# Joined-batch rows in one transfer, the last tile in one step, one x w product moved ahead

## The chip, the cores and the metric

The kernel runs on one core of a Trainium2 chip. The time is device microseconds (us) of one launch; three runs of the kernel before gave 436.42, 436.83 and 436.47 us, so its time is the median of **436.47 us**.

The engines are PE (matmul), DVE (vector), ACT (scalar), POOL (GpSimd) and SP, which only issues DMA transfers. Sixteen DMA engines move the data of all queues.

## The reference

Inputs are q, k and v of 8 batches x 8 heads x 576 positions x 64, weights `w_r` and `w_i` of 64 modes x 512 x 512, and `w_ch` of 512 x 512, all float32. Cut to what matters:

```python
rel = pos[:, None] - pos[None, :]
mask = (rel >= 0) & (rel < 64)
attn = softmax(where(mask, q @ k.T / 8, -1e9))        # sliding window, causal
x = (attn @ v) as [8, 576, 512]                       # heads side by side
X = rfft(x, axis=1)[:, :64]                           # 64 modes
Y = einsum('bmd,mde->bme', X, w_r + 1j * w_i)         # complex product
y = irfft(Y padded with zeros, n=576, axis=1)
u = x + y
out = u + maximum(u @ w_ch, 0)                        # [8, 576, 512] float32, 9.44 MB
```

## The kernel before

The work is one program with an order written out by hand (`tc.manual_schedule()`), so each engine runs its instructions in the order in which the code emits them. First comes attention, with a discrete Fourier transform of each batch as a matmul. Meanwhile and afterwards POOL's queue streams the weights `w_r` and `w_i` into rings of tiles, and `mode_half` multiplies them with the transformed x, four modes at a time. The last two groups of modes (`LAST`, `LAST + 1`) are held back as a small remainder: the outputs' share of all other modes can be prepared before them.

The output has 36 tiles of 128 rows x 512. For each batch four of them are rows 128c to 128c + 127. Rows 512 to 575 of two neighbouring batches are joined to one further tile: tiles 8, 17, 26 and 35 hold batches (0, 1), (2, 3), (4, 5) and (6, 7), the even batch in partitions 0 to 63, the odd one in partitions 64 to 127. `tiles[i]` holds the tile's x, its (column, batch) pairs and its one or two places in `out`; `tile_of` gives a tile's number.

For each tile two sums are formed in PSUM: `pu` is u = x + irfft(Y), and `ps` is u @ w_ch, made of a stored product `XW[i]` (x @ w_ch) and the transformed Z = Y @ w_ch. `tail_xw(n, js)` copies `XW` of the tiles js of pair n into `ps` with a matmul by the identity (L777); this is called the first x w product here.

The tiles go in 18 pairs, `seq`:

- n = 0 to 3: (0, 4), (1, 5), (2, 6), (3, 7);
- n = 4 to 11, alternating: (18, 19), (9, 13), (20, 21), (10, 14), (22, 23), (11, 15), (24, 25), (12, 16);
- n = 12 and 13, the joined-batch tiles, `X4`: (8, 17), (26, 35);
- n = 14 to 17, `BB`: (27, 28), (29, 30), (31, 32), (33, 34).

Tiles 0 to 7 and 9 to 16 are "early" ones. All their sums but the share of the last modes are ready beforehand, and the function `early(n)` ends them: PE adds the small remainders (L787, L794), DVE adds u (L820, `take_u`), ACT rectifies (L825) and POOL adds the two (L826, `take_z`). The others are done in full by `full_u(n)` and `full_z(n)`: PE computes the rows (L836, L840, for joined tiles L845, L859), ACT or DVE takes u from PSUM (L853, L851; for tile 28 POOL adds x, L855), and DVE rectifies and adds (L878). The last pair is done by `last(n)`, with its own DVE steps and transfers (L902, L905). Before all this, after the last weights, `zl` (L984) is the remainder's product with `w_ch` in two halves, `cast_halves` (L618, L619) takes such halves to SBUF with DVE and ACT, and pair n = 0 is written out by hand.

PSUM has eight banks in five rings, `bank(h)`: "m" two, "t" two, "z" two, "y" one, "p" one. `ps` of even pairs uses "t" and of odd pairs "z"; `pu` of even pairs uses "m", of odd pairs "y" and "p".

The output transfers follow `plan`, an order that is worked out beforehand from assumed times of each tile. SP issues the tiles in that order: ..., 11, 8, 17, 15, 26, 35, 12, 16, 27, 29, 31, 33, 34. Some transfers are given to ACT (`by_act`): the upper halves of the four joined tiles, and the whole tiles 28, 30 and 32. ACT issues them one pair later, when `full_u` or `last` of the next pair calls `send_behind` behind its own copies.

In the last pair, tile 33 is one DVE step and one transfer by SP. Tile 34 is two DVE steps of 256 columns, of which SP sends the first half and ACT the second.

Of the kernel before, what the change touches and what calls it, by code (L numbers as in the profile page):

```python
# [13 lines left out]
ALU = mybir.AluOpType  # L14
# [12 lines left out]
def kernel(  # L27
# [10 lines left out]
    nc = tc.nc  # L38
    B, H, S, D = q.shape
    NM = moe_w_r.shape[0]  # L40
    DM = moe_w_ch.shape[0]
# [7 lines left out]
    HALF = DM // 2  # L49
# [117 lines left out]
    def mode_half(psm, grp, hb, ri, first, last):  # L167
        pairs = range(4 * grp, 4 * grp + 4)
        of, p0 = (XL[hb], 4 * LAST) if grp // 2 == LAST // 2 else (XQ[hb], 0)
        order = [(j, p) for j in range(NJ) for p in pairs]  # L170
        ending = (grp, hb, ri) == (*steps[-1], 1)
        if ending:
            order.sort(key=lambda jp: (jp[1], jp[0]))
        for j, p in order:
            g = p % 4
            parts = psm if isinstance(psm, list) else [psm]
            for i, ps in enumerate(parts):
                e = DM // len(parts)
                nc.tensor.matmul(out=ps[32 * g:32 * g + 32, 0:e],  # L179
                                 lhsT=of.rearrange("k s b m -> k (s b) m")[:, (3 * j + 1 - ri) * B:(3 * j + 5 - ri) * B, p - p0],  # L180
                                 rhs=wtiles[p, hb, ri][:, j, e * i:e * i + e],
                                 start=(first and ri == 0 and j == 0), stop=(last and ri == 1 and j == NJ - 1),
                                 tile_position=(0, 32 * g))
        for p in pairs:
            wtiles.pop((p, hb, ri))
        spent.update(i for i, (_, ps, *of) in enumerate(wlist) if ps[0] in pairs and of == [hb, ri])

    with tc.manual_schedule():
# [184 lines left out]
        for nm in ("k", "q", "v"):  # L373
# [9 lines left out]
                                in1=at.unsqueeze(2).to_broadcast([128, NTF, NM]), op0=ALU.mult, op1=ALU.mult)  # L383
# [7 lines left out]
                         op0=ALU.max, op1=ALU.min)  # L391
# [141 lines left out]
        def bank(h, shape=(128, DM), dtype=FP32, name=None):  # L533
            return banks[h].tile(list(shape), dtype, name=name or "ps" + h, tag="bank")
# [196 lines left out]
        tiles = []  # L731
# [23 lines left out]
        BB = [(8, 17), (26, 35)] + [(i, i + 1) for k in range(NLB // 2, B // 2) for i in range(9 * k, 9 * k + 8, 2)]  # L755
        assert sorted(i for p in AA + BB for i in p) == list(range(NT))
        X4 = [BB.pop(0) for _ in range(2)]
        seq = [AA.pop(0) for _ in range(4)]
# [3 lines left out]
        ps, pu = {}, {}  # L762
# [9 lines left out]
        done = {}  # L772

        def tail_xw(n, js=(0, 1)):
            for i in [seq[n][j] for j in js]:
                ps[i] = bank("zt"[n % 2 == 0])
                nc.tensor.matmul(out=ps[i], lhsT=ident_r, rhs=XW[i], start=True, stop=True)  # L777

        def banks_u(n):
            for j, i in enumerate(seq[n]):  # L780
                pu[i] = bank("m" if n % 2 == 0 else "yp"[j])

        def late_u(n):
            for i in seq[n]:
                (at, b), = tiles[i][1]
                r = slice(YG[b], YG[b] + 16)
                nc.tensor.matmul(out=pu[i], lhsT=trigL[r, at:at + 128], rhs=YL[r], start=True, stop=True,  # L787
                                 tile_position=(YG[b], 0))
# [5 lines left out]
                nc.tensor.matmul(out=ps[i], lhsT=trigLr[r, at:at + 128], rhs=ZL[r], start=False, stop=True,  # L794
                                 skip_group_check=True, tile_position=(ZG[b], 0))

        by_act = {(i, 1) for p in X4 for i in p} | {(p[1], 0) for p in BB[:-1]}
        behind = []

        def send(i, ut):  # L800
            done[i] = ut
            behind.extend((i, h) for h in range(2) if (i, h) in by_act)
            while plan and plan[0] in done:
                i = plan.pop(0)
                for h in range(len(tiles[i][2])):
                    if (i, h) not in by_act:
                        put_out(nc.sync, i, h)

        def put_out(by, i, h):
            to = tiles[i][2]  # L810
            m = 128 // len(to)
            by.dma_start(out=to[h], in_=done[i][m * h:m * h + m, :])

        def send_behind():
            while behind:
                put_out(nc.scalar, *behind.pop(0))

        def take_u(n):
            for i in seq[n]:
                nc.vector.tensor_tensor(out=UE[i], in0=pu[i], in1=UE[i], op=ALU.add)  # L820
# [41 lines left out]
        uts = {}  # L862
# [17 lines left out]
                send(i, ut[:, j])  # L880

        def early(n):
            tail_xw(n)
            banks_u(n)
            late_u(n)
            late_z(n)
            take_u(n)
            take_z(n)

        def last(n):  # L890
            banks_u(n)
            ut = [ringA.tile([128, 2, DM], FP32, name="ut", tag="wt")[:, 0] for _ in range(2)]
            for j, i in enumerate(seq[n]):
                rows_u((i,))
                take_rows(i, ut[j])
            send_behind()
            for j, i in enumerate(seq[n]):
                tail_xw(n, (j,))
                rows_z(i)
                for lo in range(0, DM, HALF * (2 - j)):  # L900
                    hi = lo + HALF * (2 - j)
                    nc.vector.scalar_tensor_tensor(out=ut[j][:, lo:hi], in0=ps[i][:, lo:hi], scalar=0.0,  # L902
                                                   in1=ut[j][:, lo:hi], op0=ALU.max, op1=ALU.add)
                    by = nc.scalar if lo else nc.sync
                    by.dma_start(out=tiles[i][2][0][:, lo:hi], in_=ut[j][:, lo:hi])  # L905

        stmp2 = pool("stmp2", side="right", reuse_waits="tile")
        tables = list(inverse_tables())
# [5 lines left out]
        for i, (grp, hb) in enumerate(steps[EARLY:]):  # L914
            f, l = grp < EARLY or hb == 0, hb == 1
            if i == EARLY:
                while tables:
                    tables.pop(0)()
                while jobs or pend:
                    advance()  # L920
                close(stmp2, yp, ringB)
                Zall = pool("zall", side="right").tile([2 * NM, B, DM], FP32R, name="Zall")
                x_jobs(pool("xp1", side="right", reuse_waits="tile"), NX0, NT)
                nc.vector.memset(YT[:, :, :, rows], 0.0)
                nc.vector.tensor_scalar(out=trz.rearrange("p c g k -> p c (g k)"), scalar1=0.0, scalar2=None, op0=ALU.mult,
                                        in0=ident.unsqueeze(1).to_broadcast([128, NDCH, 128]))
                for g in range(4):
                    nc.sync.dma_start(out=trigL[32 * g:32 * g + 16], in_=trigI[rows, 0:512])
                    nc.sync.dma_start(out=trigLr.bitcast(FP32)[32 * g:32 * g + 16], in_=trigIr.bitcast(FP32)[rows, 0:512])
                given = 0  # L930
            if f:
                psm = [bank("m"), bank("m")] if grp == LAST + 1 else bank("m")
            for ri in range(2):
                if half == n0 + n1 - 2:
                    while jobs or pend:
                        advance()
                if half == n0 + n1 - 1:
                    late["first"] = bank("z")
                    late[0][1]()
                    tail_xw(0)  # L940
                mode_half(psm, grp, hb, ri, f, l)
                load_weights(len(wlist))
                while ready:
                    ready.pop(0)()
                for t in tables[0:2]:
                    t()
                del tables[0:2]
                if half == 0:
                    nc.gpsimd.dma_start(out=wch, in_=moe_w_ch.rearrange("(c p) e -> p c e", p=128))
                if l and ri:  # L950
                    finish_group(grp, psm)
                    if grp == NGRP - 1:
                        ready.pop(0)()
                        for b in range(B):
                            batch_job(b)
                            if 0 < b <= NLB:
                                early_jobs(b - 1)
                half += 1
                if half <= n0:
                    want = max(half - 4, 0) * NX0 // (n0 - 4)  # L960
                elif half <= n0 + n1 - 8:
                    want = (half - n0) * (NT - NX0) // (n1 - 8)
                else:
                    want = NT - NX0 + (half - n0 - n1 + 8) * (B + 7 * NLB) // 6
                while given < want:
                    advance()
                    given += 1
# [10 lines left out]
        YL = stgpool.tile([128, DM], BF16, name="stg")  # L978
        nc.vector.tensor_copy(out=YL, in_=first)
        take()  # L980
        zl = [bank("z"), bank("m")]
        for h, ps_ in enumerate(zl):
            for c in range(NDCH):
                nc.tensor.matmul(out=ps_[:, 0:HALF], lhsT=trz[:, c].rearrange("p g k -> p (g k)"),  # L984
# [57 lines left out]
```

## Time and profile before

| | |
|---|---|
| median of the runs | 436.47 us (436.42 to 436.83) |
| the profiled execution: its own time | 436.39 us |
| its span in the profile | 434.6 us |
| mean granted PE clock | 0.879 |
| PE busy | 339.6 us, 78% of the span |
| DVE, ACT, POOL busy | 231.7, 179.8, 144.1 us |
| software queue q0 (weights and attention inputs) | 81.73 MB, 99.7% of 16 engines' span |
| output by SP's queue | 28 transfers of 256 KB, 5 of 128 KB |
| output by ACT's queue | 3 transfers of 256 KB, 5 of 128 KB |
| last weights land, PE goes on | 397.9 us |
| last arithmetic ends | 429.3 us |

The span runs from the first to the last instruction that the profiler saw, and times inside it count from its start. A busy share is an average over stages: the weights fill the DMA queues up to about 398 us, and the part that the change touches most is what comes behind. There a line of the timeline stands for a group of instructions: its start, its length, the engine, the source line, the operation, what it writes and reads, and in brackets the idle time of the engine before it with what ended that. "SPq" and "ACTq" mark the issue of a transfer, not the transfer itself.

### The profile page before, as it was taken

Reading aid. Unit: us, or ns where it says so; the run is one execution under the profiler, and the core shown is the slowest. Engines: PE = TensorE matmul, PEld = TensorE weight load, DVE = VectorE, ACT = ScalarE, POOL = GpSimd, SP = SyncE. Lnnn points to the kernel's source line nnn. Section 1 sums busy time; section 2 is a strip of 40 time slices with the busy share of each in tenths; the row PEclk is TensorE's granted clock in tenths of the full one; section 3 lists DMA queues with packets and bytes.
Section 4 is the critical chain, followed back from the end, with each engine's and each line's share of the span. In section 5 each row is a group of like instructions: output and inputs, shape, how many; then the busy total and the mean of one; then the engine's idle time right before and its main releaser. Section 6 shows DMA issues by size and latency. Waiting matters only on the chain.

```text
span 434.6 us, 11132 instructions
## 1 busy us (share of the span) xinstructions
PE 339.6 (78%) x4758; PEld 219.3 (50%) x4802; DVE 231.7 (53%) x472; ACT 179.8 (41%) x322; POOL 144.1 (33%) x212
## 2 busy tenths in 40 slices
PE   6889989898999998986407665767696678878994
PEld 3566767676677676662103232444353345445552
DVE  8488778787677675865103111122131315662994
ACT  5566666575666667531201110121121213334842
POOL 9332323332314223223232223123332223310890
PEclk8699999999999999986558558588888989999998
DMA  8999999999999999999999999999999999993798
GB/s 205 211 211 211 212 210 210 212 210 211 211 211 211 212 212 210 211 211 211 211 258 213 216 211 211 211 211 211 211 212 212 209 211 211 211 211 71 241 367 295
DMA packets 48273, 93.65 MB, mean 215 GB/s; under 512 B 3680, under 2 KB 4128, under 8 KB 48224
## 3 DMA queue, kind: packets, MB, share of 16 engines
q0 software_dynamic: 42000, 81.73, 99.7%
q1 hardware_dynamic: 5328, 9.77, 6.4%
q10 hardware_dynamic: 896, 1.44, 1.1%
q8 instruction: 37, 0.61, 0.5%
q14 instruction: 12, 0.10, 0.1%
HBM read 163.58 MB, written 9.44 MB: 398 GB/s over the span
## 4 chain that ended last, share of the span: by engine, by line
DMA 44%; PE 38%; issue 9%; ACT 3%; DVE 3%; POOL 2%; DVEq 0%; POOLq 0%
DMA wr<-in_moe_w_r_dram 37%; PE tr L222 6%; PE s L269 5%; PE s L281 4%; PE pt L289 4%; PE vb L234 4%; DMA rawk<-in_k_dram 3%; DMA wi<-in_moe_w_i_dram 3%; PE o L309 3%; PE s L261 2%; PE psm L179 2%; POOL wi L158 1%; PE psz L777 1%; PE px L332 1%; PE pst L777 1%
## 5 line engine op out<-in xcount | busy, mean ns | idle before, releaser
L158 POOL DMA_DIRECT2D wi<-in_moe_w_i_dram x62 | 44.0, 711 | 93.0 <-PE psm L179 41.9
L601 PE MATMUL psz<-wch,tr 128*128 128x512 f32 x176 | 63.0, 491 | 11.2 <-DMA wch<-in_moe_w_ch_dram 11.0
L747 DVE CAST xw<-psz 128x512 fp32r<-128x512 f32 x36 | 24.9, 692 | 86.7 <-PE psz L601 86.1
L158 POOL DMA_DIRECT2D wr<-in_moe_w_r_dram x53 | 37.9, 716 | 83.9 <-PE psm L179 38.6
L273 DVE TENSOR_REDUCE mx<-s 128x4 fp32r<-128x512 f32 x72 | 49.5, 688 | 27.2 <-PE s L269 26.8
L575 ACT CAST tr<-ptx 128x512 fp32r<-128x512 bf16 x36 | 21.1, 587 | 103.6 <-PE ptx L594 103.6
L179 PEld LDWEIGHTS <-XQ 128*32 128x32 bf16 x448 | 20.9, 167 | 71.2 <-issue 63.8
L179 PE MATMUL psm<-wi,XQ 128*32 128x512 bf16 x212 | 28.8, 469 | 30.4 <-DMA wi<-in_moe_w_i_dram 30.4
L601 PEld LDWEIGHTS psz<-wch,tr 128*128 128x128 f32 x176 | 37.5, 236 | 18.3 <-issue 11.6
L283 ACT ACTIVATE p<-s 128x512 bf16<-128x512 f32 x72 | 39.7, 603 | 13.9 <-PE s L281 13.9
L179 PE MATMUL psm<-wr,XQ 128*32 128x512 bf16 x180 | 25.9, 497 | 17.5 <-DMA wr<-in_moe_w_r_dram 16.7
L269 PE MATMUL s<-kT,qT 64*64 64x128 bf16 (+1 forms) x576 | 29.4, 223 | 6.9 <-issue 6.9
L226 ACT COPY kT<-tr 128x576 bf16<-128x576 bf16 x32 | 23.1, 723 | 22.5 <-PE tr L222 22.5
L292 DVE COPY pts<-pt 128x1024 bf16<-128x1024 bf16 (+1 forms) x40 | 25.2, 629 | 5.9 <-PE pt L289 4.5
L226 ACT COPY qT<-tr 128x576 bf16<-128x576 bf16 x32 | 23.3, 728 | 10.5 <-PE tr L222 10.4
L269 PEld LDWEIGHTS <-qT 64*64 64x64 bf16 x576 | 18.0, 108 | 18.6 <-issue 18.0
L281 PE MATMUL s<-mx,ident_r 128*128 128x512 f32 x72 | 26.8, 445 | 0.0
L226 ACT COPY vT<-tr 128x576 bf16<-128x576 bf16 x32 | 23.3, 728 | 4.3 <-PE tr L222 4.2
L289 PE MATMUL pt<-ident_bf,p 128*128 128x128 bf16 x288 | 23.4, 220 | 2.0 <-issue 1.8
L626 DVE TENSOR_TENSOR stg<-psm,Ypair 128x512 bf16<-128x512 f32 x10 | 6.9, 690 | 33.6 <-PE psm L179 33.6
L321 DVE TENSOR_TENSOR x_sb<-o,r 128x512 bf16<-128x512 f32 x32 | 22.1, 692 | 1.1
L209 POOL DMA_DIRECT2D rawk<-in_k_dram x15 | 8.3, 556 | 39.4 <-PE tr L222 24.5
(211 smaller groups left out, 612.6 us busy)
## 6 DMA issues: line engine op xcount, KB each, us to landing
wi<-in_moe_w_i_dram POOLq DMA_DIRECT2D x60, 512.0 KB, 16.0
wr<-in_moe_w_r_dram POOLq DMA_DIRECT2D x53, 512.0 KB, 16.4
out_dram<-ut SPq DMA_DIRECT2D x28, 256.0 KB, 3.0
rawv<-in_v_dram POOLq DMA_DIRECT2D x16, 288.0 KB, 14.3
rawk<-in_k_dram POOLq DMA_DIRECT2D x15, 288.0 KB, 13.1
rawq<-in_q_dram POOLq DMA_DIRECT2D x15, 288.0 KB, 13.4
Ypair<-in_moe_w_r_dram POOLq DMA_DIRECT2D x5, 512.0 KB, 14.3
x_sb<-in_moe_w_r_dram POOLq DMA_DIRECT2D x4, 512.0 KB, 15.3
```

What stands on the lines that cost most here:

```text
L158: nc.gpsimd.dma_start(out=w[:, 0:len(ps)], in_=src[ps[0]:ps[-1] + 1, HALF * hb:HALF * hb + HALF, :].rearrange("g (p j) e -> p g j e", j=NJ))
L179: nc.tensor.matmul(out=ps[32 * g:32 * g + 32, 0:e], lhsT=of.rearrange("k s b m -> k (s b) m")[:, (3 * j + 1 - ri) * B:(3 * j + 5 - ri) * B ...
L222: nc.tensor.transpose(out=pt[ro, j, :], in_=raw[ro, TH * half + j, :], identity=ident_bf[ro, ro])
L226: nc.scalar.copy(out=to, in_=pt.rearrange("p j n -> p n j"))
L269: nc.tensor.matmul(out=s[ro, t, lo:128], lhsT=lq, rhs=kT[ro, 64 * n - 64 + lo:64 * n + 64], start=False, stop=True, skip_group_check=True)
L273: nc.vector.tensor_reduce(out=mx, in_=s, axis=AX.X, op=ALU.max, negate=True)
L281: nc.tensor.matmul(out=s, lhsT=ident_r, rhs=mx.unsqueeze(2).to_broadcast([128, 4, 128]), start=False, stop=True, skip_group_check=True)
L283: nc.scalar.activation(out=p[:, 4 * c2:4 * c2 + 4, :], in_=s, func=ACT_F.Exp, scale=EX_SCALE)
L289: nc.tensor.transpose(out=pt[:, t, :], in_=st[u]["p"][:, t, :], identity=ident_bf)
L292: nc.vector.tensor_copy(out=ps[:, 0:nt, :], in_=pt[:, 0:nt, :])
L601: nc.tensor.matmul(out=pz, lhsT=tr[:, c, :], rhs=wch[:, c, :], start=(c == 0), stop=(c == NDCH - 1))
L747: nc.vector.tensor_copy(out=XW[i], in_=multiply(tr))
```

## The change

Four things are edited.

- The joined tiles leave by pairs: one transfer of SP takes partitions 0 to 63 of both tiles of a pair (batches 0 and 2, or 4 and 6), one of ACT takes partitions 64 to 127 (batches 1 and 3, or 5 and 7). SP's is issued when the plan comes to the pair's second tile, ACT's in the next `send_behind`.
- `by_act` is gone, so tiles 28, 30 and 32 are sent by SP in the plan's order.
- The last pair: tile 34 is one DVE step of 512 columns and one transfer, by ACT.
- The first x w product of tile 1 (the first of pair n = 1) moves from `early(1)` to just ahead of the last `mode_half`, behind those of pair n = 0. It takes the second "z" bank, so the first half of `zl` takes a bank "m" in place of "z".

```diff
-        by_act = {(i, 1) for p in X4 for i in p} | {(p[1], 0) for p in BB[:-1]}
         behind = []
 
         def send(i, ut):
             done[i] = ut
-            behind.extend((i, h) for h in range(2) if (i, h) in by_act)
             while plan and plan[0] in done:
                 i = plan.pop(0)
-                for h in range(len(tiles[i][2])):
-                    if (i, h) not in by_act:
-                        put_out(nc.sync, i, h)
-
-        def put_out(by, i, h):
-            to = tiles[i][2]
-            m = 128 // len(to)
-            by.dma_start(out=to[h], in_=done[i][m * h:m * h + m, :])
+                if len(tiles[i][2]) == 1:
+                    nc.sync.dma_start(out=tiles[i][2][0], in_=done[i])
+                elif i == tiles_of_two(i)[1]:
+                    put_two(nc.sync, i, 0)
+                    behind.append(i)
+
+        def tiles_of_two(i):
+            return next(p for p in X4 if i in p)
+
+        def put_two(by, i, h):
+            p = tiles_of_two(i)
+            b = [tiles[t][1][h][1] for t in p]
+            by.dma_start(out=out[b[0]:b[1] + 1:b[1] - b[0], 512:576].rearrange("b t e -> t b e"),
+                         in_=uts[seq.index(p)][64 * h:64 * h + 64])
 
         def send_behind():
             while behind:
-                put_out(nc.scalar, *behind.pop(0))
+                put_two(nc.scalar, behind.pop(0), 1)
...
         def early(n):
-            tail_xw(n)
+            tail_xw(n, (0, 1) if n > 1 else (1,))
...
                 rows_z(i)
-                for lo in range(0, DM, HALF * (2 - j)):
-                    hi = lo + HALF * (2 - j)
-                    nc.vector.scalar_tensor_tensor(out=ut[j][:, lo:hi], in0=ps[i][:, lo:hi], scalar=0.0,
-                                                   in1=ut[j][:, lo:hi], op0=ALU.max, op1=ALU.add)
-                    by = nc.scalar if lo else nc.sync
-                    by.dma_start(out=tiles[i][2][0][:, lo:hi], in_=ut[j][:, lo:hi])
+                nc.vector.scalar_tensor_tensor(out=ut[j], in0=ps[i], scalar=0.0, in1=ut[j], op0=ALU.max, op1=ALU.add)
+                by = nc.scalar if j else nc.sync
+                by.dma_start(out=tiles[i][2][0], in_=ut[j])
...
                     late["first"] = bank("z")
                     late[0][1]()
                     tail_xw(0)
+                    tail_xw(1, (0,))
                 mode_half(psm, grp, hb, ri, f, l)
...
-        zl = [bank("z"), bank("m")]
+        zl = [bank("m"), bank("m")]
```

## The prediction

> **What bounds the kernel now.** I read the page's second part first. From the second to the 36th slice the DMA engines are over 90% busy, mostly with weights; slice 37 (71 GB/s) is the change from reading weights to writing results, and the last three slices write.
>
> ```profile
> DMA  8999999999999999999999999999999999993798
> GB/s 205 211 211 211 212 210 210 212 210 211 211 211 211 212 212 210 211 211 211 211 258 213 216 211 211 211 211 211 211 212 212 209 211 211 211 211 71 241 367 295
> ```
>
> The edit of the last weight step (the moved product) stands at 395 us, all others behind 419 us, so the second view is the windows of the end. Columns: stretch, its length, busy time of PE, PEld, DVE, ACT, POOL, then the granted clock, the DMA share and GB/s.
>
> ```profile
> 408.00:409.00 1.00, 0.95 (x9) 0.60 (x10) 1.00 (x3) 0.49 (x1) 1.00 (x2) 1.00 0.51 186
> 409.00:415.00 6.00, 6.00 (x36) 4.01 (x35) 5.36 (x10) 4.50 (x10) 6.00 (x6) 1.00 1.03 381
> 415.00:421.00 6.00, 6.00 (x32) 3.45 (x31) 5.60 (x10) 2.74 (x6) 6.00 (x6) 1.00 1.03 381
> 421.00:422.00 1.00, 1.00 (x6) 0.56 (x5) 1.00 (x2) 0.00 (x0) 1.00 (x2) 1.00 1.05 279
> 422.00:423.00 1.00, 1.00 (x6) 0.63 (x6) 1.00 (x3) 0.59 (x1) 1.00 (x1) 1.00 0.97 330
> 423.00:424.00 1.00, 0.95 (x7) 0.79 (x6) 0.90 (x2) 0.62 (x2) 1.00 (x2) 1.00 0.97 348
> 424.00:425.00 1.00, 1.00 (x8) 0.55 (x7) 0.85 (x3) 0.45 (x1) 0.20 (x1) 1.00 0.83 240
> 425.00:426.00 1.00, 1.00 (x7) 0.86 (x6) 1.00 (x2) 0.55 (x2) 0.00 (x0) 1.00 0.92 301
> 426.00:429.00 3.00, 2.33 (x13) 1.34 (x11) 2.46 (x6) 1.60 (x4) 0.00 (x0) 1.00 1.04 391
> ```
>
> PE is busy without a break until 428.3, and the chain of waits names PE there. But from 409 us on the DMA engines are full too, and they stay full (386 GB/s) from 429 to 432, when no engine computes. The timeline of the end says the same:
>
> ```profile
> 427.96 1.35 DVE L902 SCALAR_TENSOR_TENSOR ut<-psz,ut 128x512 f32<-128x512 f32 x3 [0.29 <-ACT ut L853]
> 428.68 2.27 SPq L905 DMA_DIRECT2D out_dram<-ut  x2
> 429.39 0.34 ACTq L905 DMA_DIRECT2D out_dram<-ut  x1
> ```
>
> The last arithmetic ends at 427.96 + 1.35 = 429.31, the DMA engines run to about 433, and the span is 434.6. An output transfer lands in as little as 2.3 us; the last ones need 3.7. So the end is set by the draining of result bytes, about 1.4 us behind the arithmetic, and an edit is worth what it does to that drain. The drain has one bad stretch, 421 to 426 us, in which the two pairs of joined-batch tiles (8,17) and (26,35) leave as eight transfers of 64 rows (128 KB), four from SP and four from ACT. There 300 GB/s stand against 381 before: (381 - 300) x 5 / 381 = 1.06 us lost. The DMA view splits it by queue (q1 is SP's, q10 is ACT's), first for 409 to 421, then for 421 to 426:
>
> ```profile
> q1 hardware_dynamic: 2499, 4.56, 102.7%
> ```
>
> ```profile
> q1 hardware_dynamic: 559, 0.97, 53.3%
> q10 hardware_dynamic: 316, 0.52, 41.1%
> ```
>
> A share is of 16 engines over the window. Ordinary: 1.027 x 12 x 16 / 4.56 = 43.2 us of engine time a MB. In the bad stretch SP's queue costs 0.533 x 80 / 0.97 = 44.0, with its 64-row transfers in it; ACT's costs 0.411 x 80 / 0.52 = 63.2. ACT's rows 64 to 127 are thus dear: (63.2 - 43.2) x 0.52 / 16 = **0.65 us**. The rest is idle engines: the mean share is 0.948 against 1.03, 5 x 0.082 / 1.03 = **0.40 us**. They idle while ready work stands at SP:
>
> ```profile
> 420.52 2.56 POOL L826 TENSOR_TENSOR ut<-XQ,ut 128x512 f32<-128x512 f32 x2
> ...
> 423.80 1.15 SPq L812 DMA_DIRECT2D out_dram<-ut  x1
> ```
>
> That SP row is tile 12, the first of these two POOL steps, ready near 421.8. Its transfer issues two microseconds later and takes 1.15 us to do so, behind 17's, 15's, 26's and 35's.
>
> **The change part by part.** *The joined transfers.* Eight 128 KB transfers become four of 256 KB; the same 1.05 MB from the same halves of the partitions, still lower rows by SP, upper rows by ACT. SP has 3 issues ahead of tile 12 from (8,17) on where it had 5, and each carries the bytes of an ordinary tile, so its queue should stay as full as in 409 to 421, where transfers of 256 KB alone kept it at 381 GB/s. I take the 0.40 us of idle engines as regained (bounds: 0, and a loss if the joined form is dearer, below). The dear rows of ACT stay: no row shows why they are dear, and their number doesn't change; 0.65 us stays (bounds: all regained, or SP's rows as dear). The joined form adds a wait: tile 8's rows wait for tile 17's DVE step, 0.65 us later (L878 takes 1.28 for two). Behind it on SP stand 15, 12 and 16, but the second half-transfer stood in the same place with the same wait, so they wait no longer than now; and SP's queue then still holds tile 11. On ACT the joined transfer of (26,35) waits until 422.7, as 35's does now, with the copy of tile 29 (423.38) behind it.
>
> *Tiles 28, 30, 32 from ACT to SP.* SP then sends all tiles before the last; its issue count from tile 8 on is 11 before (8, 17, 15, 26, 35, 12, 16, 27, 29, 31, 33) plus half of 34, 12, and after it 2 + 3 + 7 = 12. One queue alone moved 381 GB/s, two moved 391 (426 to 429). Over 4 us that is 1.56 / 0.381 - 1.56 / 0.391 = **0.10 us** lost. ACT loses three issues between its copies, which helps nobody: PE doesn't wait there.
>
> *The last tile.* DVE: one step of 0.68 for two of 0.33 to 0.35; the end of arithmetic stays at 429.3. SP's half was issued late, at 429.79, as SP was still busy with tile 33; now all leaves by ACT at about 429.4. With the engines full until 432 an earlier issue is worth nothing by itself. Packets of 1 KB become 2 KB: 432 to 433 us, mostly 1 KB packets, has 0.803 x 16 / 0.27 = 47.6 us a MB against 43.2, for 0.26 MB: **0.07 us** won.
>
> *The moved product.* PE loses one product of x and w (0.47 for a pair at full clock, so 0.23) from the row of n = 1, at 402.3, and gets it at about 396, where it stands 0.72 us idle ahead of the last matmuls for the last weights (L179, released by the DMA at 397.9): hidden, 0.23 if the weights came early. At 402 it is not on the path either, as ACT's rectifying steps follow one another without a gap, and PE waits for the banks that they free:
>
> ```profile
> 402.44 1.09 ACT L825 ACTIVATE ut<-pst 128x512 f32<-128x512 f32 x2
> 403.43 1.08 ACT L825 ACTIVATE ut<-psz 128x512 f32<-128x512 f32 x2
> 404.54 1.08 ACT L825 ACTIVATE ut<-pst 128x512 f32<-128x512 f32 x2
> ```
>
> The first two pairs of outputs go through POOL from 403.1 on, which starts behind the product of n = 0 as before. Value 0, at most 0.23, and hidden by the drain even then. The second bank "m" for `zl` comes free with the casts of the last group (398.9), before L984 at 399.7; the banks of n = 0 come free with the casts of `zl` (400.9, 401.4), before L787 at 401.8: nothing.
>
> *Sum.* -0.40 + 0.10 - 0.07 = -0.37 us. The profiled execution took 436.39 (434.61 and 1.78 around it), 0.08 under the median of 436.47; the median falls to **436.1**. 0.2% is 0.87 us, about what a measurement of this kernel can tell from no change.
>
> **The rivals.** *B: the whole bad stretch goes.* If ACT's rows are dear because its half transfers ran with little beside them, full queues on both sides cure that too: -1.06 + 0.10 - 0.07 = -1.03, and 435.4. For: 421.5 to 422 is the dearest half microsecond, with q10 alone at work (48 packets, 97.8% of the engines, 163 ns each, 217 GB/s). Against: from 424 to 425.5, with q1 at work too, q10's 122 packets still took 53.0% of 16 engines, 104 ns with the tiny ones counted. Only with the stretch nearly gone is it faster by over 0.87.
>
> *C: slower.* A joined transfer takes two packets from each of 64 partitions. If this makes both queues' rows as dear as ACT's worst (163 ns for 2 KB, 79.6 us a MB), the stretch loses (79.6 - 43.2) x 1.05 / 16 = 2.39 us for 1.06: +1.33 + 0.03, 437.8. It decides from a mean of 72 us a MB over all four transfers. Against: SP's lower rows show no surcharge at all. For: the transfer into few partitions, `Zall` (16 rows of the tile, 256 KB), needed 4.2 us to land where an output early in the tail needs 2.3 to 2.9.
>
> *D: nothing is regained.* The stretch runs at the rate of 64-row transfers whatever their number: 436.47 + 0.03 = 436.5. For: 64 rows are all that is special in the stretch; against, SP's cheap ones. [...]
>
> **How the numbers follow.** The forecast, idle engines regained and dear rows kept, 0.45, 436.1; B 0.27, 435.4; D 0.18, 436.5; C 0.10, 437.8. Forecast and D are within 0.2%: 0.63; B is faster: 0.27 (it and a little of the moved product); C is slower: 0.10. The range leaves out C's upper part: from B with 0.23 of the product and the scatter of runs, 435.0, to 437.0, half of C's price.
>
> **What would show it.** Right: DMA share over 1.0 through the stretch, q10 still over 55 us a MB, SP's long issue near 424 gone or earlier, 380 GB/s on q1 to the end, last arithmetic at 429.3 and the DMA end some 0.4 us earlier. Wrong: idle engines in the stretch still (D), q10 near 43 us a MB (B), q1 over 60 (C), or arithmetic that ends at another time than 429.3.

## The result, and the profile after

The changed kernel takes **437.47 us** (median of 20 runs, 436.82 to 437.79); the kernel before took 436.59 us in the same comparison (20 runs, 436.10 to 437.51). The ratio is 1.0019, 95% interval 1.0012 to 1.0026: slower by 0.9 us, where 436.1 and a range of 435.0 to 437.0 were forecast. The profiled execution took 437.57 us with a span of 435.8, 1.2 us more than the span before.

The page's second part, same two lines: up to the last slices nothing differs; slice 37 to 40 show the writing of results, with a lower rate in slice 39 (326 for 367 GB/s).

```profile
DMA  8999999999999999999999999999999999992898
GB/s 206 211 211 211 212 211 211 210 211 211 211 211 211 211 211 211 211 211 211 212 258 212 216 211 211 211 211 211 211 211 211 211 211 211 211 209 59 276 326 291
```

The windows of the end, after (stretch, length, busy time of PE, PEld, DVE, ACT, POOL, granted clock, DMA share, GB/s):

```profile
415.00:421.00 6.00, 6.00 (x31) 3.46 (x31) 5.60 (x10) 2.67 (x6) 6.00 (x6) 1.00 1.03 381
421.00:422.00 1.00, 1.00 (x6) 0.53 (x5) 1.00 (x3) 0.03 (x1) 1.00 (x2) 1.00 0.74 207
422.00:423.00 1.00, 1.00 (x6) 0.65 (x6) 1.00 (x3) 0.56 (x1) 1.00 (x2) 1.00 0.98 186
423.00:424.00 1.00, 0.95 (x6) 0.76 (x5) 0.90 (x2) 0.63 (x2) 1.00 (x1) 1.00 1.00 244
424.00:425.00 1.00, 1.00 (x7) 0.58 (x6) 0.89 (x3) 0.45 (x1) 0.10 (x1) 1.00 0.93 275
425.00:426.00 1.00, 1.00 (x7) 0.86 (x6) 1.00 (x2) 0.84 (x2) 0.00 (x0) 1.00 1.00 283
426.00:427.00 1.00, 1.00 (x9) 0.56 (x8) 0.70 (x3) 0.31 (x2) 0.00 (x0) 1.00 1.00 287
427.00:428.00 1.00, 1.00 (x7) 0.71 (x4) 0.71 (x3) 1.00 (x2) 0.00 (x0) 1.00 0.91 301
428.00:431.00 3.00, 0.26 (x2) 0.00 (x0) 1.18 (x2) 0.01 (x1) 0.00 (x0) 1.00 1.04 390
433.00:434.00 1.00, 0.00 (x0) 0.00 (x0) 0.00 (x0) 0.00 (x0) 0.00 (x0) 0.50 0.87 330
```

Up to 421 us the two kernels are alike. Then the bad stretch is both longer (to 428 instead of 426) and lower. The loss against 381 GB/s is now (381 - 255) x 7 / 381 = 2.3 us, 255 GB/s being the mean of the seven rows; it was 1.06. The engines still write at 330 GB/s at 433 us, when the kernel before was done. The timeline shows that arithmetic isn't late: it ends at 427.89 + 1.29 = 429.2 (429.3 before).

```profile
427.89 1.29 DVE L904 SCALAR_TENSOR_TENSOR ut<-psz,ut 128x512 f32<-128x512 f32 x2 [0.29 <-issue]
429.21 0.36 ACTq L906 DMA_DIRECT2D out_dram<-ut  x1
431.82 0.78 SPq L906 DMA_DIRECT2D out_dram<-ut  x1
```

The DMA view of 421 to 428 us by queue (packets, MB, share of 16 engines), after:

```profile
q1 hardware_dynamic: 686, 1.25, 63.4%
q10 hardware_dynamic: 288, 0.52, 30.2%
```

SP's queue costs 0.634 x 112 / 1.25 = 56.8 us of engine time a MB, where it was at 44.0 before; ACT's costs 65.0 (63.2 before). The shares add up to 0.94 against 1.03: 0.62 us of idle engines, for 0.40. So SP's rows are dear here, as rival C had it (though just under the 60 named as its sign), and the idle time grew. How dear a joined transfer is shows between 421.6 and 422.9 us, where one is alone:

```profile
DMA packets 119, 0.24 MB, mean 186 GB/s; under 512 B 1, under 2 KB 1, under 8 KB 119
q1 hardware_dynamic: 119, 0.24, 96.5%
```

0.965 x 1.3 x 16 / 119 = 169 ns a packet of 2 KB; an ordinary one takes 43.2 us a MB x 2 KB = 88 ns. ACT's joined transfer isn't there yet, though it was issued in the same moment:

```profile
420.26 0.67 SPq L815 DMA_DIRECT2D out_dram<-ut  x1
420.26 0.72 ACTq L815 DMA_DIRECT2D out_dram<-ut  x1
```

### The profile page after: what moved, and what is told of

Same layout as the page of the kernel before. It is cut to its first block, busy times and chain, and to the rows that moved or that the text cites. A ratio compares the mean times of both kernels' runs of the same rounds, so it can differ in the third digit from the quotient of the medians.

```text
span 435.8 us, 11120 instructions
## 1 busy us (share of the span) xinstructions
PE 340.4 (78%) x4758; PEld 220.5 (51%) x4802; DVE 230.9 (53%) x471; ACT 179.7 (41%) x322; POOL 144.0 (33%) x212
## 4 chain that ended last, share of the span: by engine, by line
DMA 48%; PE 35%; issue 8%; ACT 3%; DVE 2%; POOL 1%; DVEq 0%; POOLq 0%
DMA wi<-in_moe_w_i_dram 33%; DMA wr<-in_moe_w_r_dram 7%; PE tr L222 6%; PE s L269 5%; DMA Yall<-in_moe_w_i_dram 4%; DMA rawk<-in_k_dram 4%; PE pt L289 4%; PE s L281 3%; PE vb L234 3%; PE o L309 2%; PE s L261 2%; PE psm L179 2%; PE psz L777 1%; PE pst L777 1%; PE pst L863 1%
## 5 line engine op out<-in xcount | busy, mean ns | idle before, releaser
L179 PE MATMUL psm<-wi,XQ 128*32 128x512 bf16 x212 | 29.9, 475 | 28.6 <-DMA wi<-in_moe_w_i_dram 28.6
L179 PE MATMUL psm<-wr,XQ 128*32 128x512 bf16 x180 | 24.9, 491 | 17.2 <-DMA wr<-in_moe_w_r_dram 16.6
L222 PE MATMUL tr<-ident_bf,rawk 64*64 64x64 bf16 x576 | 15.6, 197 | 5.3 <-DMA rawk<-in_k_dram 3.3
```

The source lines that it names most:

```text
L179: nc.tensor.matmul(out=ps[32 * g:32 * g + 32, 0:e], lhsT=of.rearrange("k s b m -> k (s b) m")[:, (3 * j + 1 - ri) * B:(3 * j + 5 - ri) * B ...
L222: nc.tensor.transpose(out=pt[ro, j, :], in_=raw[ro, TH * half + j, :], identity=ident_bf[ro, ro])
```

## The experiments

All kernels are the kernel before with the edit shown, unless said otherwise. A ratio is against the kernel before on the same chip.

### One edit at a time

**The joined transfers alone** (the other edits left out):

```diff
-        by_act = {(i, 1) for p in X4 for i in p} | {(p[1], 0) for p in BB[:-1]}
+        by_act = {(p[1], h) for p in X4 for h in (1,)} | {(p[1], 0) for p in BB[:-1]}
+        two = {i: p for p in X4 for i in p}
...
-                    if (i, h) not in by_act:
+                    if (i, h) not in by_act and not (i in two and (h or i == two[i][0])):
...
+            if i in two:
+                b = [tiles[t][1][h][1] for t in two[i]]
+                by.dma_start(out=out[b[0]:b[1] + 1:b[1] - b[0], 512:576].rearrange("b t e -> t b e"),
+                             in_=uts[seq.index(two[i])][64 * h:64 * h + 64])
+                return
```

> The kernel before with the four joined transfers alone (lower rows by SP, upper rows by ACT); 28, 30 and 32 stay on ACT, the last tile stays in two halves. Theory 1 (the joined transfers are the whole loss): the stretch from 421 us runs near 255 GB/s for about 7 us as in the changed kernel, both queues over 55 us of engine time a MB there, and the kernel is slower by 0.8 to 1.3 us (ratio 1.002 to 1.003). Theory 2 (the loss comes from giving SP all other tiles): within 0.3 us of the kernel before, the stretch near 300 GB/s.

Measured: 437.90 us, ratio 1.0032 (1.0020 to 1.0045): 1.3 us slower, at the upper end of what theory 1 gave. The stretch is there again: 274 GB/s over 421 to 428 us, with both queues at 56 us of engine time a MB. Its first rows:

```profile
421.00:422.00 1.00, 1.00 (x7) 0.56 (x5) 1.00 (x3) 0.00 (x0) 1.00 (x1) 1.00 0.79 283
422.00:423.00 1.00, 1.00 (x6) 0.64 (x4) 1.00 (x3) 0.59 (x1) 1.00 (x2) 1.00 0.99 195
423.00:424.00 1.00, 1.00 (x8) 0.79 (x8) 0.90 (x2) 0.25 (x1) 1.00 (x2) 1.00 0.99 236
424.00:425.00 1.00, 1.00 (x7) 0.63 (x6) 0.86 (x2) 0.83 (x2) 0.48 (x1) 1.00 0.92 252
```

**The changed kernel with only the joined transfers undone** (eight half transfers again, the other three edits kept):

```diff
-                elif i == tiles_of_two(i)[1]:
-                    put_two(nc.sync, i, 0)
-                    behind.append(i)
+                else:
+                    put_half(nc.sync, i, 0)
+                    behind.append(i)
...
-                put_two(nc.scalar, behind.pop(0), 1)
+                put_half(nc.scalar, behind.pop(0), 1)
```

> The changed kernel with the joined transfers alone undone: eight half transfers again, lower by SP and upper by ACT; 28, 30 and 32 on SP, the last tile in one step and the moved product stay. Theory 1 (the joined transfers are the whole loss): within 0.3 us of the kernel before, ratio 0.9995 to 1.0005, the stretch near 300 GB/s. Theory 2 (the other three edits): as slow as the changed kernel, ratio 1.0019.

Measured: 436.59 us, ratio 0.9999 (0.9990 to 1.0008), and 307 GB/s from 421 to 426 us, close to the 300 of the kernel before. With the joined transfers the loss comes, without them it goes: theory 1. The three other edits by themselves:

**The moved product** (`tail_xw(1, (0,))` ahead of the last `mode_half`, `zl` in two "m" banks):

> The kernel before with the moved x w product alone (and the bank of zl with it). All theories: no effect over 0.1 us at the end, since ACT's rectifying steps pace the first pairs and the output transfers drain until 433 us; the first output transfer leaves about 0.1 us earlier, as in the changed kernel (404.34 against 404.43), and ratio 1.000 within 0.0005. If the product did cost something, this run alone would be slower by over 0.3 us.

Measured: ratio 1.0002 (0.9993 to 1.0010). The first output transfer was issued at 404.51 us, not earlier than before.

**The last tile** (one DVE step, one transfer by ACT):

> The kernel before with the last tile in one DVE step and one transfer by ACT alone. Theory 1 (the joined transfers are the whole loss): between -0.2 and +0.1 us, the last packet near 433.1. Theory 2 (the loss is at the end of the queues, where tile 33 waits on SP's queue until 431.8 us in the changed kernel): +0.3 us or more already here.

Measured: ratio 1.0001 (0.9993 to 1.0010). The DMA engines were done shortly after 433 us (0.04 busy from 433 to 434).

**Tiles 28, 30, 32 by SP** (`| {(p[1], 0) for p in BB[:-1]}` dropped):

> The kernel before with tiles 28, 30 and 32 sent by SP alone; the joined-batch tiles keep their eight half transfers. Theory 1: +0.1 us at most, 381 GB/s on one queue against 391 on two. Theory 2: slower by 0.8 to 1.2 us, as SP's issues of over 1 us each delay the last tiles.

Measured: ratio 1.0003 (0.9994 to 1.0012). None of the three can be told from no change; the bounds are 0.4 to 0.5 us, so the forecast's 0.07 and 0.10 us are neither confirmed nor refuted. Theory 2 falls. The joined transfers alone cost more (1.0032) than the whole change (1.0019), but the intervals overlap: whether the other edits give a little back beside them stays open.

### What makes a joined transfer dear

A joined transfer differs from an ordinary one in two ways: it takes two packets from each partition, and it takes them out of one half of the partitions. The next runs separate the two on the steady stretch from 409 to 421 us, where the kernel before has 43.2 us of engine time a MB, with tiles 18 to 25.

**Two packets a partition, all 128 partitions:**

```diff
+            nc.sync.dma_start(out=out[4 + b, 128 * c:128 * c + 256].rearrange("(j t) e -> t j e", j=2), in_=uts[n])
```

> The kernel before, with the tile pairs (18,19), (20,21), (22,23), (24,25) sent as one transfer each: two packets of 2 KB from each of all 128 partitions, 512 KB. It has the joined form, but not the half set of partitions. Theory H (one half of the partitions alone is the slow thing): 43 to 45 us of engine time a MB from 409 to 421 us and 375 to 385 GB/s, as before. Theory F (two packets from each partition are slow in themselves): over 55 us a MB in the mean of that window, under 330 GB/s.

**64 rows in the plain form, grouped by half:**

```diff
+            for h in range(2):
+                for i in seq[n]:
+                    nc.sync.dma_start(out=tiles[i][2][0][64 * h:64 * h + 64], in_=done[i][64 * h:64 * h + 64, :])
```

> The kernel before, with the same eight tiles sent as 64-row transfers in the plain form (one packet a partition), grouped by half: lower rows of both tiles, then upper rows of both, all by SP. Theory H: two lower ones in a row leave the upper partitions idle; these 2.1 MB cost 60 to 80 us a MB, so over 409 to 421 us the mean is 50 to 58 us a MB and the rate 290 to 340 GB/s. Theory F: 43 to 45 us a MB, 375 to 385 GB/s.

**The same transfers, lower and upper rows in turn** (the two loops exchanged):

> As the grouped run, but alternating: lower and upper rows of the first tile, then of the second. The same 32 transfers at the same times. Theory H: neighbours in the queue take turns between the halves and overlap, so the price lies well under the grouped run's, 44 to 52 us a MB. Theory F: 43 to 45 us a MB, as in the grouped run. If both runs are dear alike, it is neither, but the number of 64-row transfers.

The DMA view of 409 to 421 us, in this order:

```profile
q1 hardware_dynamic: 2360, 4.43, 100.1%
```

```profile
q1 hardware_dynamic: 1923, 3.34, 94.1%
```

```profile
q1 hardware_dynamic: 1925, 3.36, 94.4%
```

With 12 x 16 = 192 us of engine time that is 43.4, 54.1 and 53.9 us a MB. Two packets a partition cost nothing here (43.4 for 43.2; theory F falls), and 64-row transfers are dear in the plain form too. But the alternating run isn't cheaper than the grouped one, as theory H had expected: on one queue, taking turns brought nothing (53.9 for 54.1). The expectation had named what this would mean, that dear might be the small number of rows and not the half. (Each of the three ran once, 437.32, 440.91 and 441.64 us, where the kernel before has a median of 436.69 on the same chip. Their rates over the window, 370, 279 and 280 GB/s, lie 5 to 11 GB/s under what theory H gave for the first two.) Two more runs settle that. They cut the same eight tiles into three pieces each, one of 64 rows and two of 32 (the second run has `((0, 32), (32, 96), (96, 128))` in the same place):

```diff
+            for i in seq[n]:
+                for lo, hi in ((0, 64), (64, 96), (96, 128)):
+                    nc.sync.dma_start(out=tiles[i][2][0][lo:hi], in_=done[i][lo:hi, :])
```

> The kernel before, with tiles 18 to 25 sent in three pieces each by SP: rows 0 to 63, 64 to 95, 96 to 127. Companion of the next run, with the same number and sizes of pieces. Theory H (transfers out of one half of the partitions are dear): 56 to 64 us of engine time a MB over 409 to 421 us. Theory N (dear is the small number of rows in a transfer, wherever they lie): the same as the next run, within 2 us a MB.

> As the run before, but cut into rows 0 to 31, 32 to 95 and 96 to 127: the 64-row piece now takes 32 partitions from each half. Theory H: that piece costs the ordinary 43 to 46 us a MB, so the mean over 409 to 421 us lies 4 us a MB or more under the companion run's. Theory N: the same as the companion within 2 us a MB.

Over 409 to 421 us, cut at 64 first, cut at 32 and 96 second:

```profile
q1 hardware_dynamic: 1721, 2.82, 78.9%
```

```profile
q1 hardware_dynamic: 1707, 2.81, 72.7%
```

53.7 and 49.7 us a MB: 4.0 apart, just at the expected limit, though the first is below its own forecast of 56. (Each ran once, 444.12 and 444.55 us. The six pieces of a pair take SP 3.3 us to issue and leave the DMA engines partly idle, so these times say nothing of the half.) The 64-row pieces themselves are clear. A window that lies inside one, rows 0 to 63 (409.9 to 410.4 us) first, rows 32 to 95 (410.35 to 410.7) second:

```profile
DMA packets 56, 0.11 MB, mean 217 GB/s; under 512 B 3, under 2 KB 3, under 8 KB 56
q1 hardware_dynamic: 56, 0.11, 104.2%
```

```profile
DMA packets 62, 0.11 MB, mean 328 GB/s; under 512 B 6, under 2 KB 6, under 8 KB 62
q1 hardware_dynamic: 62, 0.11, 88.1%
```

Without the tiny packets (those under 512 B): 1.042 x 0.5 x 16 / 53 = 157 ns against 0.881 x 0.35 x 16 / 56 = 88 ns. Two windows six microseconds later, 415.85 to 416.45 and 416.37 to 416.75, give 162 and 88 ns. The same number of rows, the same form, the same queue: out of one half of the partitions a packet took 1.8 times as long (157 and 162 ns), out of 32 of each half it took what an ordinary one does (88 ns). Theory H holds, N falls. Why a packet out of one half takes longer, no run here shows.

### An attempt at a better order

If a half transfer wastes engine time, it might be sent where the engines are half idle, ahead of 409 us (0.51 busy from 408 to 409 in the kernel before):

```diff
-        while AA:
-            seq += [BB.pop(0), AA.pop(0)]
-        seq += X4 + BB
+        mid = X4 + [BB.pop(0) for _ in range(2)]
+        while AA:
+            seq += [mid.pop(0), AA.pop(0)]
+        seq += BB
```

> The kernel before with the joined-batch pairs (8,17) and (26,35) as n = 4 and 6 of the order, ahead of (18,19), so that their eight half transfers leave from about 408 us, where the DMA engines are half idle, and (22,23), (24,25) move to the end. If what counts is engine time that the 64-row transfers waste while the queues are full (theory H), part of the 1.06 us is hidden: -0.3 to -0.9 us, ratio 0.998 to 0.9993, and the window from 421 to 426 us runs at 380 GB/s or more. Rival: the early place only moves the waste, as the queues fill from 409 us on anyway: ratio 0.9995 to 1.0005 with the slow stretch at 409 to 414 us.

Measured: 439.02 us, ratio 1.0058 (1.0045 to 1.0071): slower by 2.4 us. Both expectations missed a new wait, which the timeline names:

```profile
424.10 0.69 DVE L879 SCALAR_TENSOR_TENSOR ut<-pst,ut 128x512 f32<-128x512 f32 x1 [3.68 <-POOL ut L856]
```

`add_x` gives POOL the x of the second tile of the first remaining pair, which is now tile 23 at n = 12, while POOL still has the early tiles in its queue; DVE waits 3.7 us for it. From 424 to 427 us the DMA engines are only 0.65 busy (240 GB/s), and the last arithmetic ends at 433.6 us, 4.3 us later than in the kernel before. The window from 412 to 415 us at 285 GB/s says besides that the waste had moved there and wasn't hidden. A version with the addition elsewhere wasn't run, so how much of the 2.4 us is this wait, and what the early place alone is worth, stay open. No version here beat the kernel before.

## Why the prediction was wrong, point by point

- **What bounds the end: right.** The arithmetic ended 0.1 us earlier and the kernel 0.9 us later; the time went where the DMA engines' drain went.
- **"I take the 0.40 us of idle engines as regained": wrong.** Idle time grew to 0.62 us. Part of it is the added wait that the prediction dismissed: SP's transfer for tiles 8 and 17 was issued at 420.26 and its first bytes found emptying engines, 0.74 busy and 207 GB/s from 421 to 422 us, where the kernel before had sent tile 8's half at 419.79 and kept 1.05 and 279. "SP's queue then still holds tile 11" covered less time than the wait needed.
- **"SP's lower rows show no surcharge": the step that failed.** SP's 44.0 us a MB was right as a number, but it was read as a property of the lower rows, and no other trace bears that out. Four traces here have the same eight half transfers between 421 and 426 us. SP's queue costs 56.8 us a MB and ACT's 47.5 with the moved product alone, 55.7 and 48.3 with the last tile alone, 52.5 and 48.3 with 28, 30 and 32 by SP, 51.8 and 52.0 with the joined transfers undone. The first of them:

```profile
q1 hardware_dynamic: 556, 0.95, 67.4%
q10 hardware_dynamic: 266, 0.45, 26.7%
```

Over both queues together it is 50.7 in the kernel before and 51.1 to 53.8 in these four. The queue that started while the other moved next to nothing was the dear one: ACT's in the kernel before (163 ns a packet from 421.5 to 422 us), SP's in the four others (with the moved product 1.107 x 0.45 x 16 / 48 = 166 ns from 421.6 to 422.05 us). So lower rows were as dear as upper ones when they went alone, 157 to 169 ns a packet. The forecast kept the 0.65 us of dear rows where the changed kernel has (56.8 - 43.2) x 1.25 / 16 + (65.0 - 43.2) x 0.52 / 16 = 1.06 + 0.71 = 1.77 us.

- **Rival C: near in its size, by luck, and its reason half right.** It put the stretch at 2.39 us and the time at 437.8; measured were 1.77 + 0.62 = 2.39 us by the shares (2.3 by the rates) and 437.47 us. The agreement is luck: C had all of it from dear rows and nothing from idle engines, and the 65.0 us a MB of ACT's two joined transfers is less than the 72 that C asked for. It also blamed the two packets from each partition, which the 512 KB run acquits (43.4 us a MB); it is the half set of partitions (157 ns a packet for rows 0 to 63, 88 ns for rows 32 to 95). The trace had the row for the half set, the half microsecond with ACT's queue alone at 217 GB/s; B and C both used it, but the sum went by SP's cheap rows. C got 0.10 and the range stopped at half of its price.
- **Rival D** took one rate for 64-row transfers and drew "no change", since both kernels send them. The stretch had no such common rate: 300 GB/s in the kernel before and 255 in the kernel after, 1.06 and 2.3 us lost. The 64 rows were also not what is dear: rows 32 to 95 took the ordinary 88 ns a packet. What it missed besides is that the halves ran beside each other in part. Counted along each queue in the packet records of the traces, a packet of the eight half transfers takes 106 ns in the mean in the kernel before and 109 to 113 ns in the four traces above; one of the four joined transfers takes 138 ns in the changed kernel and 132 ns in the run with them alone; 64-row transfers of SP's queue alone, grouped or alternating, take 131 ns (tiles 18 to 23), and an ordinary tile's 87 to 88. The first two joined transfers ran almost one behind the other.
- **The moved product, the last tile, 28, 30 and 32 by SP: right as far as can be told,** each within 0.03% and with bounds of some 0.1%; together, without the joined transfers, 0.9999.

What stays open: why ACT's joined transfer, issued together with SP's, sent nothing until SP's was nearly done. That it did is shown; nothing was run to find its cause. So it is also open whether four joined transfers overlap less than eight halves because each is twice as long, or because both of a pair are issued at once and only when its second tile is ready.

## What to carry to other kernels

Merging transfers need not be a gain: here eight transfers made into four went from 106 to 138 ns a packet. Ask which partitions are being read at each moment (157 ns a packet for rows 0 to 63 alone, 88 ns for rows 32 to 95), not only how many transfers there are. A price read from a queue's row holds for what ran beside it in that one execution (SP's 44.0 us a MB was 51.8 to 56.8 in four other traces); before it is carried to another arrangement, look for a window where that traffic was alone, and read the same rows in a second trace. When an engine's end isn't the kernel's end (here the arithmetic ended 0.1 us earlier and the kernel 0.9 us later), cost each edit in the resource that drains last.

## What the runs showed of the hardware that was not expected

- A transfer out of 64 partitions at one end of the tile moved 186 to 218 GB/s while it was alone, 157 to 169 ns a 2 KB packet, and one out of partitions 32 to 95 took the ordinary 88 ns.
- Two 256 KB transfers issued by SP and ACT at the same 420.26 us, one from each half, did not overlap at first: SP's had the engines to itself from 421.6 to 422.9 us.
- Half transfers of both halves from two queues, SP's and ACT's, moved 285 GB/s from 421.9 to 423.2 us with the joined transfers undone, so they overlapped in part; such halves in turn on SP's queue alone moved 203 GB/s from 409.9 to 412.4 us in the alternating run.
- Transfers of 512 KB with two packets from each of 128 partitions left the window from 409 to 421 us at 43.4 us of engine time a MB, where transfers of 256 KB alone had 43.2.
